# A written-out order of 2757 operations, replaced by another one: four transformer-like layers on one core

## The chip, the cores and the metric

The kernel runs on one core of one Trainium2 chip. The metric is device time in microseconds of one execution: the median of several runs. A core has five instruction queues that run side by side and meet only at semaphores: PE (TensorE, the matrix unit; its weight loads are shown apart as PEld), DVE (VectorE), ACT (ScalarE), POOL (GpSimd), and SP (SyncE), which in this kernel issues nearly all DMAs.

## The reference

The input is X, 2048 rows of 512 numbers (bf16). It passes through A, B, A, B, each with a residual: x + A(layernorm(x)), x + B(layernorm(x)). Both have 32 heads of 16 numbers.

```python
# A: causal attention inside each segment of 512 rows, and a linear memory of the earlier ones
for s in range(4):
    p = softmax(qs @ ks.T * scale + mask)
    a_dot = p @ vs
    a_mem = (phi(qs) @ M) / (phi(qs) @ z + 1e-6)     # phi(t) = t + 1 if t > 0 else exp(t)
    o = g * a_mem + (1 - g) * a_dot
    M = M + phi(ks).T @ vs;  z = z + sum(phi(ks))
# B: linear attention over all 2048 rows
pq, pk = q @ w_phi, k @ w_phi
phi_q, phi_k = [softmax(pq), softmax(-pq)], [softmax(pk), softmax(-pk)]
o = (phi_q @ (phi_k.T @ v)) / (phi_q @ sum(phi_k) + 1e-6)
# each ends with o @ wo
```

## The kernel before, in words

X stays on the chip as 16 tiles of 128 rows. A segment s (of 0 to 3) is four tiles, and L (0 or 1) counts the two A-and-B pairs. Segments of the second pair are called xA4 to xA7 in this text where their transposed input is meant, so xA5 is segment 1 of L = 1.

*Normalisation and transpose* (`ln`, line 574 on). Each tile gets its mean and variance on DVE, a reciprocal root on POOL (on ACT for the first four tiles), and a normalised copy `xn` on DVE or ACT (line 597 on DVE). Then the copy is transposed into a tile of `pX`, which holds one segment: by PE for some tiles, by a DMA transpose on SP (`tr`, line 364) for the others. The segment-1 tiles of the first pair, 4 to 7, go by DMA.

*Projections* (`a_proj`, matmuls at line 341 through `pair`). A segment's transposed input times the key, query and value weights (`WA_k`, `WA_q`, `WA_v`), two groups of four heads' pairs at a time. Keys are copied from PSUM (`Kev`) and written four times with masks (`kmask`, line 647, tile `KM`), so that one matmul can take several heads; queries are copied (`Qev`) into `QT`. The value tile is copied into `pV`, and two DMAs (line 736) make a copy with swapped halves, `pW`. For the memory, phi of the keys is transposed by DMA and multiplied with the values (`Macc`, `Mmask`).

*Attention* (`a_att`). A block is two tiles of query rows (i0 = 0 or 2) of one segment: 16 blocks in the whole kernel. For each of four head groups PE makes score groups in PSUM (line 326, tiles `pK` and `pQ`), ACT takes an exponential of each of them (line 351, some 0.8 to 1.0 us each; `exp`, `expf`, `expd`), and PE multiplies the result with the values. The causal mask is added by one matmul of `tri` with `two`. DVE divides, adds the memory's part, the result is transposed (mostly by DMA), multiplied with `WA_o` and added to X (line 925).

*Linear attention* (`b_keys` after each segment, `b_query` for each segment after the last). The key and query weights of B are folded with `w_phi` on the chip (`fold_weights`): raw weights are loaded, transposed by DMA on SP, multiplied, and copied. `Zev` copies the query normaliser out of PSUM.

*Order.* The program first lists all operations with what they read and write (`Graph.op`). Nothing schedules them as the kernel runs, and nothing plans them as it is built: the table `ORDER`, a compressed string, holds one sequence of all 2757 operations, an engine for each operation, and a buffer number for each tile. `Graph.place` (line 137) reads it and refuses an order in which an operation stands ahead of one that it needs, or a tile ahead of the end of the last user of its buffer; `Graph.emit` cuts the sequence into the five queues and puts a semaphore wait where an operation needs one on another engine. Each engine works through its queue strictly in the table's order. Buffer pools are small: five tiles of `pX` (used for xA, xB and raw weights), four PSUM tiles of 128 x 1024 (`pD`), 22 of 128 x 1024 in bf16 (`p2`).

On SP the head of the queue is, in this order: X tiles 2 and 3, X 4 to 7, the two halves of `WA_k`, beta, two parts of `WB_o`, a half of `WA_q`, a part of `WA_o`, `WB_o`, `WA_o`, `WA_v`, X 8 to 11, the transpose of tile 7, X 12 to 15, the transpose of tile 5, the raw value weights (512 KB), the transpose of tile 4, the raw key weights (512 KB), and the transpose of tile 6.

Of the kernel before, what the change touches and what calls it, by code (L numbers as in the profile page):

```python
# [16 lines left out]
D = 512  # L17
H = 32
# [3 lines left out]
NG = 4  # L22
# [275 lines left out]
class Kernel:  # L298
# [147 lines left out]
    def T(self, pool, cls):  # L446
        return Tile(pool, cls)
# [727 lines left out]
YY-J&>lKKN9Y8dp$l|{_>chNK|)9h3KBs|NCpU1p)3F}RD+^W4vK*T0s$IgKx~i@1d$L37OF#Wr~xIQJmiI%kPq@h0jK~ap%#>af>03(K_#dSb)XxRhVD=X3PWZ19;  # L1175
!eO=n1``2#kbuFbYOPdYA^|U;^}prO*dPz#DiA26Dk2$O)<7G2DfBkQTmy_wX(J08ii^+=r)-9iBlBcmXfr0gQzVkQ*k#c*qLRVGMi)51}u-f&w@gmqC9R0Lx($yoM
oI5C_3F7>*-wJB-B5PzXoi8YqlgU=s9$fv^LHz)BblA@Cz~#p%!yyJ07s0b5}*{DP}tEzE>Zm=VHZD0~fJ@CZWTJJ<=k;ByFu0LXz^@F!RTIWa3{!=GU&YRrzqushC
!9%yh51n~!$4XYqAWCM%Eu^8sTT$m4YV^7SBQy@R~!jJF^Oobvi7KcG+EQ;fBK74}VumDQnI+z83nV=-@h9tNLRzOnhi+dp%B6dNC<FOx3z~nd@*I)`9gKKdWPR0Q^
1?R#-U|bJ`De)UzjU#9gOvK*UA4gIjTnyi0W+;tia07gY-{VG@gzIoWl*a=w2-jl;+<*g7^9uwz2!?;aH~11QBfZ6`m<OieaUeq8h&8bm#>J{w4a;IVjEC{@M-0F$@
CuKCz&bbsD`7>PiPf<(*1#$ljKiol*2Q|b1w-&NI0>n-6xK)L2ABYc(^lMuoA4Zj;yXMKU%+<Uj7#tg%%U$L63@a<_%nXMKum-QF@pC&I39u%FdZAB#E;0d6lc>;+=  # L1180
cUS2QI=!I3E||9Gr`daRDyGCK!eh7=%sH@oRjKvv4=g#%WZTmSII&i7T)ORiYWR95d2%nn`nLE@h$sPK<jn2JXdRZibnuIkv!-7|E^i2(-ZvW^Rj7+zv<4XevwjC_j
~>0u)A@s32{o;uKDWs67^?Q&55g6{9FTM2AVzX^5bhs4xOzLMq&ct*`?s+Cckp5N)K&RE5e@NjiX$RDl9$FvY?%co0uuAjP1Q_!)kVhwv~4Q4BtUr*Ive#ZnXpW8-=
{hhu0geSzty8l|VIG>%GB8OlJRd=v#&ry4Y#T2d>@fXyi*wxBdPfhJN~JcgMtiX^AQwlsv=QB#^iQ)wtQqq<a&CR2TCO>L+F)uzVOgw{|UYDn{_5ly1Clo`)sdaOx?
j)JByu|0L5j&vH2V<5+cT9lPK(R{j&3uqB7p&NJsFXAO!NQ>zv-p1s#ly=ZEN<rIbIqjsBbQm1PBuim@3-90xT1hdvGaaEWbQibNQCdY^DVS#S9KMVr`3inUqj(E_P
O)eo#ina`72{BRN<?v~8}*^S6a`u6B7{&Z4rj&paVs65{j`Vn(lI(n$7wg6pa(dbAL2>6hhum;pQY1Og3r({n!zQx9G{}cn2^fzBTP-_C;^?Pew3XnaSkrVmAN>_=A
j&ib8=$pPCckU^`s;em*dfD8pbm@5vQVAT!AZcVt$Upc?5rj@i_^np|3F+SLbSc8In>c72%>>maFnaeu4*i5?A3e{1nG?DK5>2cmk)TUi1ZhNzbqb51^Xdo7QtKUdS
7G5%1^xe1HpZZXU~Xc`8riaa@q+aUssb11T9@g2J4Tlkx?c!bkZSFXknDkuFg@zDc*J887F_JfEBMU~a%GcmX%$AzY8^^D<t`OSu(i;C0-Z5AzYO#VdIgU#8W3g%WT
b&d8fN6W8VYw1pdUBW}ShxeY&{w%ml<aZ_&3pL0r1#hLjbo#MyTNHi9==_*~LJ9L+>Qx;CnDYyf7<W8KLbJ0o8O?fCi-++z$8E2#Hw3RQwJ*v(5xHISFSg?j~&?deK
X*nzBphxtC&hl|S#|^|bKEVw|7v9NTc{}gor?i82b189}&+uLj5c{~acus+$f~Y9=a5<5a(s4HK#(nubf5H8@KM&wE{3Uni9^8|A@mCZfz9uWmi)R!moQM)J#6ZqV-
_W<zn_p0v2p2Eu6@`d6B2;K$#4Q*mVu{!ySOkff;yW5H>WB+Gi2LwucujG|_Y_ZD<hr7sxWvswebHQ8<|}-QuW~g(qJ@y+4Y8;$9&jb`kcDU|DvP(IL=(|QT!U*IUt  # L1190
EXVe4X#`UB1UPMGetblo5~k9W@nC_&rq-Wkpr-1C0`+MQhPX)Do>kVo_T><)7$BYA4!@&LW9ODw2s`D4|FsK2d4`e1jiz8j)UP5XnVKkxKkbX~hTXA~J~-BBMwrGK(
zYBV`rYM0Sxt+~=E|Lv$76#1;6O$BPM~hj_+c@kG&6Jm+utD)bRAd4%XIMv52wEx+P!qPr*|a*AFemw3&+#rIrNbP%~k9+6iR5^p%4$S(?r!s0tFB8rM)Vvv|Bn#g{
lzZfE#$^l}q7$b&?vEnT^lkfQ*H<ts&4?IOo7L&w}{8UU6)5Q!iQ*;z@pr9x&W{GEFwpb$Oh@bdp{=iGcbMcj!E9Qx1V!l`|R)_^+p;#$aiI2QaeB$+DyZD6{iN#{I
SR>Yo4Pui3u~BRmD9(tpVuxrU&xtR@VX<2r5qm^SxkYRh+r&|^SL_$(#ZIwH>=OsXA#qR~7stex;)1v+E{P86vgoKDidM3<ydqAB&&5e`N<0!*#WnGnxFhb0)8d}EE
^de?@}_toZj1ZkmguB9tH<JN@j`qno``S6OYus)7T<~Q#T(H^eiTn-TiIT=lRt=GL<jjy{wO-ix1y7LC!WjB^1b*Zy2!8O*HX$h3S?XLja0I${7H0^D1R1Ceh^xID_
_f3@`ZdUhs*9VK=zO$<ae^C43uM}kz*yvAlXiRFRf(RU%rv;)c`qCj*{bKupBRid@DobXgNXllD%c9MAcnc)m3#--Bg&IC@0A{GF--$?_`7=DBsI?GE&BuQ8JB8E0f
3=GO0`_)5`=hrpzFJkO^fnnOvrj8D&c8R1Za}r}|O$Qa{N=GL}pw6U)gmwfrD6$=Gs`{8?s}ALVovtg^^KDyy8K2CIUyiYz3v$q<!W7M6WvZ`D_>lmUv>FEW?>Bv;8
m)ko!&*<}v7TCS0cWM37kgjy@B%E7Xq93t<l1bV0pQ;TIkHB45M4^%?^wW=;N=^FC3`bK5e{nZ^cKoya9)jd^I7L%ZYlvGRPQn^g7lQrcOIa^MZbL3n(P0o|k<#IVt
<&}A42{~VulIvwHSzCsyr)s!TDxKD9gi5cUsfu#EnxIz58FGP~DUF(`O3LDLq?)BhsWNh*oFyyC%JPMZr@vJZD!zWMzEY7Yk$$8K>zC@WdZnJIhbpnoprcei8AH8R-
>JQ_h|Z`>>U}ba&ZSG~q&m0WAY-cia-y1~hNz(`g-)sC=#4V2F0QZ3Ec%8lp|k2MvbHWQ>*)AuliVzC%48~=zACTD{IY<YtVXM0>U(ut&Q@FHHhD`<QQ37eom_91Q&  # L1200
nDFN9NHvbSj-jr`2_3PJKYWQ>pcPHBD`iWo0>8PbOD8Wm=U^tyKxsFY1#Tqh9K<iu5bZI=}uw<<mRlI8{KeQw8;p>WzA<=BVm=u98~l8X7d}pVjyJC-qU4)=F#rLCs
UUWO|iBB~*#jdX+-OQYqC2HD7I1TU176bSh<aY_&|y({FScJzt-fWpz1SUVkBr>I%A;J|g3&#44_;FO#S*<srFMZByG-O<hYLl^0}1U0E;Em2_3TSXa}_)dICpEmFt
iXEL?gp$^JSYLmJocgsD}>7*)+DlaR@%qpHLqyzK<9jF)T&*dFiMX%C#WsqL1?#b19jb5vl>ScPlUZI!hx_YBtsT=AIdc9t!>*@Nsk#3+*%M&tEpOib*ad}EEQJeH;
eOKSpP4sQuKsMG5Wix$WH`T#9N*|VuWQdM$n(G!iRL9UU^$N98h3UpJmOdjd%F8lb-_do{1D(LU*N=5w^+f-mU+XODJN;I_(^*wLl}*jmv-E8JRL{``)lEHD-_p-?Z
uPT%t_!J{=7au9$1?TRL)}0XR(aJHokO+M=j3J;q0h?LdX;LZ9_erN11Zfz`9goKizsCt$vo=5T&?n{oa#p%*L>8i^iMjTiEUczIHs5?s@muRs*&2N^Q!<8Xg=w0^)
3zOfY#<0y<7Lx2emOr^ikbQ_tu?t7u{B)X{WpDZo0khpvmM?9d&lqT_4hibzfao9oN;=F?~XB(<k)~-A7kf{q%OdQ#Vn2^$OEe?a?dEe!Wj8HO<r@o!Ioyo%Cn=bIs
<Iek_ZtnyRrnt#_$4YN_h4lNoD*%wRoGCo#chfOck>PG}OD;ktwhGb41k8KrBeA$q7Tsgj!%CennMk-C&RqgR=;I@IhitIbXmWn!47rkP1)mYI|$!n8G`^*McBmsMZ
r)FzE7qe`o^X1Ten+MDL)ifU)Z=oY4<>0rj{PUf0gVy>&DrktvvuByxWhN`8m=-TRmX=6H@)~2!PYPy*&=74!<nwZ_{pxI;gnmwwOS!Y_BL#n(=XN1|Sx|<$mz1d|B
tNx~**=+`x`evMNVA7j==Dt~Ej;Mp`kU4BJn8hZeIiM=49A=+6X119v=D0ay_M7eItQoHxnxkfonV^rVwWg8DWG3pIW|FR?zSI}=MV;AfFdNM|v&n2VL(O?J%p5Vj&
# [61 lines left out]
```

## Time and profile before

| | before |
|---|---|
| median of 3 runs | 477.54 us (476.16 to 478.46) |
| profiled execution, its own time | 477.2 us |
| span of the profiled execution | 475.5 us |
| mean granted TensorE clock | 0.996 of full speed |
| busy: PE, ACT, DVE, POOL | 450.5, 424.1, 418.5, 54.7 us |

The profile is of one execution. The span runs from its first instruction to its last; the execution's own time has 1.7 us more around it. An engine is busy while it works on an instruction; a share of the span is a mean over stages that are limited by different things, so it has to be read stage by stage. In rows of single instructions the number in brackets is the idle time of that engine just ahead of it, and after the arrow stands the engine, tile and line that the profile holds for the last thing waited for. A wait for several things is put down to the one that came last by its records.

### The profile page before, as it was taken

Reading aid. Unit: us, or ns where it says so; the run is one execution under the profiler, and the core shown is the slowest. Engines: PE = TensorE matmul, PEld = TensorE weight load, DVE = VectorE, ACT = ScalarE, POOL = GpSimd, SP = SyncE. Lnnn points to the kernel's source line nnn. Section 1 sums busy time; section 2 is a strip of 40 time slices with the busy share of each in tenths; the row PEclk is TensorE's granted clock in tenths of the full one; section 3 lists DMA queues with packets and bytes.
Section 4 is the critical chain, followed back from the end, with each engine's and each line's share of the span. In section 5 each row is a group of like instructions: output and inputs, shape, how many; then the busy total and the mean of one; then the engine's idle time right before and its main releaser. Section 6 shows DMA issues by size and latency. Waiting matters only on the chain.

```text
span 475.5 us, 25072 instructions
## 1 busy us (share of the span) xinstructions
PE 450.5 (95%) x11583; PEld 296.2 (62%) x11583; DVE 418.5 (88%) x812; ACT 424.1 (89%) x567; POOL 54.7 (12%) x139
## 2 busy tenths in 40 slices
PE   9979999999999999999999999999999999999885
PEld 4447665767667676565555666666666667666542
DVE  6969999999699888987999998998897887898994
ACT  3869999999999998579999999999999999786961
POOL 2301112001011101100220041110020020110000
PEclk9989999999999999999999999999999999999999
DMA  9941292352423132100133334343104404100256
GB/s 233 248 84 39 42 127 56 76 66 48 69 51 60 25 42 33 24 1 4 37 80 70 81 47 72 69 71 59 26 5 81 61 4 70 37 12 3 55 81 204
DMA packets 89388, 30.36 MB, mean 64 GB/s; under 512 B 75954, under 2 KB 89282, under 8 KB 89282
## 3 DMA queue, kind: packets, MB, share of 16 engines
q1 hardware_dynamic: 88450, 28.20, 32.0%
q8 instruction: 91, 1.49, 1.3%
q10 hardware_dynamic: 800, 0.52, 0.4%
q14 instruction: 15, 0.12, 0.1%
q0 software_dynamic: 32, 0.02, 0.0%
HBM read 6.31 MB, written 2.10 MB: 18 GB/s over the span
## 4 chain that ended last, share of the span: by engine, by line
PE 64%; ACT 21%; DVE 12%; issue 2%; POOL 1%; DVEq 0%
PE D L341 40%; PE D L326 21%; ACT p L351 10%; ACT pF L351 7%; ACT pE L351 3%; DVE p L1087 2%; PE D L662 2%; DVE p L1084 2%; DVE X L925 1%; DVE p L360 1%; DVE p L1090 1%; DVE pT L1007 1%; DVE pK L360 1%; PE D L378 1%; DVE pV L360 1%
## 5 line engine op out<-in xcount | busy, mean ns | idle before, releaser
L351 ACT ACTIVATE p<-D 128x1024 bf16<-128x1024 f32 (+1 forms) x220 | 217.5, 1018 | 12.8 <-PE D L341 7.8
L351 ACT ACTIVATE pF<-D 128x896 bf16<-128x896 f32 x128 | 115.7, 927 | 5.1 <-PE D L326 4.5
L326 PE MATMUL D<-pK,pQ 64*128 64x256 bf16 (+3 forms) x1536 | 113.7, 243 | 4.3 <-ACT pF L351 1.9
L326 PEld LDWEIGHTS D<-pK,pQ 64*128 64x128 bf16 x1536 | 55.4, 94 | 40.8 <-ACT p L351 5.2
L326 PE MATMUL D<-pV,pF 64*128 64x34 bf16 x1024 | 76.5, 176 | 1.6 <-issue 0.8
L326 PE MATMUL D<-pW,pF 64*128 64x34 bf16 x1024 | 73.9, 176 | 0.0
L326 PEld LDWEIGHTS D<-pV,pF 64*128 64x128 bf16 x1024 | 57.2, 93 | 5.8 <-ACT pF L351 2.1
L588 POOL TENSOR_SCALAR rstd<-mv 128x1 f32<-128x1 f32 x60 | 15.0, 256 | 359.7 <-DVE mv L581 359.5
L326 PEld LDWEIGHTS D<-pW,pF 64*128 64x128 bf16 x1024 | 53.5, 93 | 1.4
L326 PE MATMUL D<-pV,p 64*128 64x34 bf16 x1024 | 53.1, 176 | 0.6 <-issue 0.2
L351 ACT ACTIVATE pE<-D 128x768 bf16<-128x768 f32 x64 | 52.1, 821 | 1.5 <-PE D L326 0.9
L326 PE MATMUL D<-pW,p 64*128 64x34 bf16 x1024 | 51.7, 176 | 0.0
L326 PEld LDWEIGHTS D<-pV,p 64*128 64x128 bf16 x1024 | 47.0, 93 | 3.3 <-issue 0.7
L326 PEld LDWEIGHTS D<-pW,p 64*128 64x128 bf16 x1024 | 45.4, 93 | 1.6
L326 PE MATMUL D<-tri,two 64*128 64x128 bf16 (+1 forms) x384 | 46.2, 234 | 0.2 <-issue 0.2
L326 PE MATMUL D<-pV,pE 64*128 64x34 bf16 x512 | 45.0, 175 | 0.0
L580 DVE BATCH_NORM_STATS2 stats<-X 128x6 f32<-128x512 bf16 x64 | 43.2, 682 | 2.0 <-DMA X<-in_A_x_dram 1.7
L326 PE MATMUL D<-pW,pE 64*128 64x34 bf16 x512 | 43.2, 175 | 0.3 <-issue 0.3
L341 PE MATMUL D<-pX,WA_k 64*128 64x512 bf16 x256 | 37.3, 383 | 2.8 <-ACT pF L351 2.6
L972 DVE TENSOR_REDUCE pS<-p 128x64 f32<-128x1024 bf16 (+1 forms) x36 | 38.5, 1090 | 1.4 <-ACT p L351 1.2
L925 DVE TENSOR_TENSOR X<-X,D 128x1024 bf16<-128x1024 bf16 (+1 forms) x29 | 32.0, 1107 | 8.4 <-PE D L341 8.3
L341 PE MATMUL D<-pX,WA_q 64*128 64x512 bf16 x256 | 37.6, 384 | 0.6 <-DVE pV L360 0.5
(132 smaller groups left out, 992.3 us busy)
## 6 DMA issues: line engine op xcount, KB each, us to landing
pW<-pV SPq DMA_DIRECT2D x16, 136.0 KB, 3.6
out_dram<-X SPq DMA_DIRECT2D x7, 256.0 KB, 4.2
X<-in_A_x_dram SPq DMA_DIRECT2D x3, 512.0 KB, 5.7
pX<-in_B_wqkv_dram SPq DMA_DIRECT2D x3, 512.0 KB, 5.0
p<-p SPq DMA_TRANSPOSE x76, 2.7
pX<-p SPq DMA_TRANSPOSE x54, 3.3
WA_k<-in_A_wk_dram SPq DMA_DIRECT2D x2, 256.0 KB, 6.8
WB_o<-in_B_wo_dram SPq DMA_DIRECT2D x8, 64.0 KB, 3.6
```

The source lines that it names most:

```text
L326: ins = e.matmul(out_ap, lhsT, rhs, start=st, stop=sp, tile_position=(basep(lhsT), basep(out_ap)))
L341: ins = e.matmul(out_ap, lhsT[64 * hf:64 * hf + 64], rhs[64 * hf:64 * hf + 64], start=k == 0 and i == 0, stop=k == 1 and i == len(lists[hf ...
L351: return self.g.op({"act": (dur, lambda e: e.activation(out_ap(), in_ap(), func, scale=scale))}, reads, writes, opens, label=label)
L360: "dve": ((340 if fast else n / 0.96 + 65), lambda e: e.tensor_copy(out_ap(), in_ap()))}
L378: ins = e.transpose(pb()[:, k * 128:(k + 1) * 128], src()[:, k * 128:(k + 1) * 128], self.ident[:])
L580: v(lambda e: e.bn_stats(self.stats[:, t, :], self.X[:, t, :]), 602, [R("X", t)], [R("st", t)], label="bn")
L588: v(lambda e: e.tensor_scalar(rs, self.mv[:, t, 1:2], LN_EPS, None, op0=ALU.add), 170, [R("mv", t)], [R("rstd", t)], eng="pool", label="rstd")
L662: ins = e.matmul(D.t[c0:, r0 * 8:r0 * 8 + n], r[:, c0:], ones(r, n), start=True, stop=True, tile_position=(r0, c0))
L925: self.v(lambda e: e.tensor_tensor(X(), X(), src(), ALU.add), 65 + 512 * n / 0.96, pr + xr, xr, label="res")
L972: fn = lambda e, sgn=sgn, eo=eo, Z=Z, n=n: e.tensor_reduce(Z.t[:, 0:64 * n].rearrange("p (k s h) -> p k s h", k=n, s=2)[:, :, sgn, :], eo( ...
L1084: v(lambda e, Ns=Ns, Tm=Tm, w=w, shape=shape: e.tensor_tensor(shape(Tm.t[:]), shape(Ns.t[:]), w(), ALU.mult), 600, [Ns, AB[0], AB[1]], [Tm ...
L1087: v(lambda e, N=N, Tm=Tm, w=w, shape=shape: e.tensor_tensor(shape(Tm.t[:]), shape(N.t[:]), w(), ALU.mult), 1131, [N, AB[0], AB[1]], [Tm], ...
```

## The change

The table is replaced; not a line of the program differs otherwise. In both tables each operation stands once, and the count per queue is the same: 1055 on PE, 812 on DVE, 568 on ACT, 187 on SP, 135 on POOL.

What differs in the decoded tables:

- Fourteen operations change between DVE and ACT, seven each way. From DVE to ACT: two evacuations of PE transposes (`xnTe`, one in each pair's first segment), the normalised copy of tile 3, two key copies `Kev` (segments 0 and 1 of the first pair), one `Macc`, and the `Zev` of the last segment. From ACT to DVE: two `xnTe`, one mask piece `Km`, two query copies `Qev`, one `Kev` in the second pair, and one of the last residual evacuations (`res`).
- Within a queue an operation moves by 2.1 places on average on PE (35 at most), 1.4 on ACT, 5.2 on DVE (78 at most), 2.6 on POOL and 4.3 on SP (65 at most).
- The head of SP's queue becomes: X 2 and 3, beta, X 4 to 7, a half of `WA_k`, `WA_v`, the other half of `WA_k`, a half of `WA_q`, X 12 to 15, X 8 to 11, the transposes of tiles 5, 7, 6 and 4, then the raw key weights, two `pW` copies, parts of `WB_o` and `WA_o`, the raw query weights and the transposes of raw key weights. The raw value weights go from place 16 to place 33.
- On PE, the first score group of rows 2 and 3 of segment 0 (third head group) goes ahead of the key projection of segment 1, and its exponential ahead of another one on ACT.
- In segment xA5 the normalisations of tiles 36 and 39 (tiles 4 and 7 of X in the second pair) stand behind 2.1 and 5.6 us more work on DVE; in xA6 two stand behind 5.2 and 6.2 us more; in xA3 the last one behind some 6 us less.

```diff
 ORDER = """
-c-rlH1GHt=vUXwmSZ&+3ZQHhO+qP}nM$$~$HiJge2)fh%+WRDV$-T+D_l@zt@ngKT_gQnzxvFYbeO2>YYmR-ALkdU(bs;q*fqGCM8bCv61dX8yG=*l+99lq2Xa%jI4
...
+c-rlH1Gr_!w(dZATW#C6ZQHhO+qP}nwvslJ?xc;Nku-vSbFJOU3C_9qyzhJW>AQ39wdSmvRipm#kAI9+bFZBoQa~E03-zErG=PTC2pU6tXaY^488n9$&=Oif5=a0EK
...
 """
```

More of the change, by code (lines that the diff above doesn't have):

```diff
@@ L1178 @@
[L1178 to L1193, printed above, removed]
@@ new lines @@
+=V>BJdEtfeerc9zi^K3{M~%WQ5o7Eqn=2;SJn{GB6TG!DyHOW8oS606)S#_zto|4wwexU_5*Uxxhef$O&&@3`~OF&<Fa$_wWw-!$24TOJOh;!euZ73*#Vo317ni=m*
+Q;K5T+*&=p7Gc31<Wup0*PO2`U3U^Q%p;Wz@fKmja>TOkCV!wOghLtr8dhFAC=Ucmzhg`KbqI^uN5fmv_{bi$mN6=%W{m<_+;T3Cgv@dISTpI|6z%#Pi07|w$pXmB$
+83`4=<I>?K8Fdyc}+?WfCV^16g<FN=9!=l&=C*WutgAV7zdKeCXC2$r@fvHdulVD%m4P$W+B*g{rEBpd`A(-btKU{;!aU3G9#m<-lKf*#thI4^2CBDNhH~>e`B%Fx7
+aRc<nk<<q_LTOwC>u?ah#}~L5%HVq359RRy48#ps0ViWwoPrxM69ghMab`FOS>PjngRhZrDt^G9@LT*2r(sQui{-EuR>f*K1LNUL{2q@(1joln{uwm~U}da=)v*Rv!
@@ new lines @@
+a7(RgRvqmz`9ru=U@U1!TM;p0Rka0hj1vr!6^O#V=z%DMnWJ&zzMhtC*c&tg4B2#N?`y5K`>0mhPV*t;wHQRTW~XO#m`_HehxA4B5cQDbPmqLa9V=9aTm_Roj8q_;(
+VM=jc^vtrp7o6BQOyr#2+yxhht*g2LhXTu7<%&`~~0QY+R0ua2f8vid2{u;|g4fqo@)Uq0y9)X3$K^L_v56!muf}#y!{!EjPy&=y)$iVjFCW?JzU7#P(R0%27TFqx=
++w1?UVEq&YN~&O#vyr=qlpiqU3@AVI~c1Z^Nm8%g3mOocHqfMeky+K+?i0CvDu7zbmcLPdFCFdf7bcnDA8VK_{Y6hKv|6qTgXRG!XZ8Cpjb=sb?0YP6oxQB|r;>FEN
+FrO#25p~G06YS1Y>jTz_&9!0?|sTDP+G?*60Q41PR>F^ky!3;QoGGaSwOG9WPWx_C?LUm~>4W)Y2l$y~bnoPB+4%MeN)SA{%LuyP7s0lTqd9;=?V-OvIK&nX>@iROM
@@ new lines @@
+mvBC{rw-JSqDZo(U^)h8@i^9^P85qnDK5l@KvtZE!ucjHpj)_z7Se58OkZGfT1F{o8!e&bw1bw?cG^OhaVKr1JD8GUkfRl}l2X%`*qLT?7dk>+sSjPjIee7v;#C~Uq
+xc%`qgZr|V$)Z+pN>-;x`Ey3I(DbNlpbSJ59&w#sV5DfRn&_v!4=p=yXh32roD86_Rs-3OJ`^_pQM8{hVS9mIGyif2|h>XX$F_%gp{3&aSl#E@u)YgrmPe~5AgwBpw
+B2Le@=-gE*0lg6q_q?WuD1#cqq@}VH}s^Qz9<M<vB4|;EMbdhx0QW!AUqiKga4^jf-$muF40w3?Jf0IFTRYB#y^vC?O}~wDbfA(nX2`rTHkA<tluP^Yd6P#fhl~*W@
+HrfXDH8&czFPF6ZV6yol#<L7vR(c`6s;X}p1xavm<s3HTE2=L6h~FH>_~%u{$iFXt<ioCos|PQghj3NAx3iUCWw0k7Z%+>q;WeO|_`cqy;t4BVR6@nO!$b$BJO;;WR
@@ new lines @@
+2uhDh7K{qK2*W%iIo9@sN-pqCRE84<sxGlHfmi#p}=BC_8wBttHgxhmUPQ{t|J~b8(sRMW9PQ02=^GUu1srd`~l5WEpKE=7{IOnEpw2@EnCeBWI=q_dD^qhkp&?CxA
+IVlZy=38`+)^I+~%R6}&U*L1Rl^ck&yp6l?cHYhBxuGa0y7CTwOyxx>v5)s~fY{63xI6dY&-in;qO=GUPsxdAR6$e}&nZGgi6;~(Vu)`kOoWT?=z9tgp(3`>!iZPYm
+wWO>?#F5Q8|u%!xHk{rf&7B9aV!y2+<_obM+A#6ARWgM!^9=N%!9ZOzofV#o~SE^i+bV;R}xqG8eiwvR9{pUB&vyKLJAhu#n;?I2+>@$6mRH0-+*iIfR(rj@x=|k$=
+Bfrdc<u+P0>~~5j8{^(NvTbKhj&OBHqy`QB{l<twk%*Nz@ieMJ@4|@9-D=CEw)_^qy|<J#Hu3i_RjU_?420L?W?BB0f@T0sN4EqVyt-$RJXP<RX<wD}JUfB9q7{Qi^
@@ new lines @@
+mUv&bTTp%LN<cNJMhHj!N<5MS|a&LN(2H!)7U;F01PcNgQuQ~s8};R)h9o+x^W-r{@iBl?OdqJ$VAriz^6CBNp9qJwzFJw#8DOXL=XL>^IC<P~qYh$t%ZiTt9NC?J~
+1exj)yBl?T6Vvraj28zMr9S;?g#U$~bAB$;Xx|ktmijJbVC@7lAAGo>vk>Bzx@kGoPOT--U6Mx{R;+goFmx{S!o>(U4iv?n#ST0tGMdBA;CqD9ev0ePiE5$0YSj2?Y
+VvSfUHi%6E#741Mpg1SaixzT+xF9|kTf|neO&k`x#SyVbw3J81Ua?<X6g$N(u}>Tj2gM<AOk5VnMF(|7+!t3xN7YKUme<4yaax=dXT$^XnYbiwi0k5%_)^>zXT?2nQ
+`{1d<Zbb__(I$fUx`ktvwA2ViEqTW;)QrFz7yYzcCxMfMZ6TR#B1?J{3;&HHnP2ZB0I<*L`V6fcqZQoDWA(u^1V><seB>dijShR{NQc;P<D}BWjFbgXrq1>T6UM;NG
@@ L1233 @@
+QnsjX)R!BV6r^(fDRCsa@B-ojF&Ctq;FL&c#UH(oM_c)2Jvc!St@xGhIog#Q6-6`vv
 """
```

80 lines of the change are left out of this document (38 added, 42 removed).

## The prediction

> **What bounds the kernel now.** I read the page's totals first, then the busy times of six stretches, which I cut where the character of the work changes, and last the instruction rows of the one stretch with idle time in it. In the stretch rows the columns are: window, its length, busy time and (instructions) of PE, PEld, DVE, ACT and POOL, the granted TensorE clock, the DMA share and GB/s.
>
> ```profile
> span 475.5 us, 25072 instructions
> PE 450.5 (95%) x11583; PEld 296.2 (62%) x11583; DVE 418.5 (88%) x812; ACT 424.1 (89%) x567; POOL 54.7 (12%) x139
> ...
> 0.00:40.00 40.00, 35.88 (x491) 19.46 (x493) 31.11 (x93) 26.92 (x43) 7.09 (x27) 0.96 0.73 168
> 40.00:180.00 140.00, 135.14 (x3986) 94.89 (x3982) 126.24 (x225) 138.18 (x178) 16.38 (x40) 1.00 0.36 60
> 180.00:220.00 40.00, 39.13 (x878) 24.40 (x876) 34.21 (x64) 30.10 (x45) 3.14 (x8) 1.00 0.11 18
> 220.00:400.00 180.00, 173.56 (x4796) 116.63 (x4792) 163.01 (x322) 177.26 (x228) 25.02 (x56) 1.00 0.30 53
> 400.00:440.00 40.00, 39.64 (x864) 25.40 (x860) 35.50 (x60) 31.01 (x44) 3.06 (x8) 1.00 0.14 25
> 440.00:475.50 35.50, 27.19 (x598) 15.43 (x592) 28.45 (x53) 20.63 (x34) 0.00 (x0) 0.99 0.49 114
> ```
>
> PE has the largest total, but in the two long stretches ACT is the full engine: 138.18 of 140 us and 177.26 of 180. In 180 to 220 and 400 to 440 PE is full and ACT has 9.9 and 9.0 us to spare. Only the first 40 us are short of both, and only there is the clock below 0.99. As the next stretch is bound by ACT, a microsecond that ACT gains in the first 40 is carried along, until a later wait eats it.
>
> The loss in the first 40 us sits in one place. The next rows are windows around it, then PE's, ACT's and DVE's instructions there (start, length, engine and line, operation, tiles; in brackets the idle time ahead of it and what the profile names as its end).
>
> ```profile
> 23.70:26.40 2.70, 0.05 (x4) 0.04 (x3) 2.12 (x7) 1.70 (x3) 0.00 (x0) 1.00 1.05 177
> 27.70:31.20 3.50, 3.50 (x22) 1.69 (x20) 1.97 (x5) 2.46 (x3) 0.00 (x0) 0.51 0.49 111
> ...
> 23.52 0.22 PE L326 MATMUL D<-tri,two 64*128 64x128 bf16 x2
> 26.39 1.04 PE L341 MATMUL D<-pX,WA_k 64*128 64x512 bf16 x8 [2.65 <-ACT pF L351]
> 29.39 1.92 PE L341 MATMUL D<-pX,WA_q 64*128 64x512 bf16 x8
> 31.37 1.04 PE L341 MATMUL D<-pX,WA_q 64*128 64x512 bf16 x8
> ...
> 27.71 0.92 ACT L351 ACTIVATE pF<-D 128x896 bf16<-128x896 f32 x1 [2.32 <-PE D L326]
> 29.66 1.02 ACT L351 ACTIVATE p<-D 128x1024 bf16<-128x1024 f32 x1 [1.03 <-PE D L326]
> 31.56 1.02 ACT L351 ACTIVATE p<-D 128x1024 bf16<-128x1024 f32 x1 [0.36 <-PE D L326]
> 33.20 2.54 ACT L351 ACTIVATE pF<-D 128x896 bf16<-128x896 f32 x3 [0.62 <-PE D L326]
> ...
> 29.23 1.23 DVE L360 CAST p<-D 128x1024 bf16<-128x1024 f32 x1 [3.41 <-PE D L341]
> ```
>
> PE stands still for 2.65 us ahead of the key projection of segment 1, and then runs at a granted clock of 0.51 for 3.5 us (the same eight matmuls take 1.92 us there and 1.04 after). ACT loses 2.32 + 1.03 + 0.36 + 0.62 = 4.33 us behind it, DVE at least 3.41. The profile names an exp as the releaser, but that projection also needs the transpose of the last tile of segment 1, which SP issues:
>
> ```profile
> 14.63 0.57 SPq L457 DMA_DIRECT2D X<-in_A_x_dram  x1
> 17.14 0.59 SPq L457 DMA_DIRECT2D pX<-in_B_wqkv_dram  x1
> 19.01 0.58 SPq L457 DMA_DIRECT2D pX<-in_B_wqkv_dram  x1
> 19.64 1.32 SPq L364 DMA_TRANSPOSE pX<-p  x1
> ...
> pX<-in_B_wqkv_dram SPq DMA_DIRECT2D x2, 512.0 KB, 5.1
> pX<-p SPq DMA_TRANSPOSE x1, 6.5
> pX<-pX SPq DMA_TRANSPOSE x2, 2.5
> ```
>
> The first four rows are SP's instructions, the last three the medians from issue to landing. The transpose issued at 19.64 landed 6.5 us later, at about 26.2, which is when PE went on (26.39). With nothing large ahead of it, two transposes from 27 us on landed in 2.5. Ahead of it stood two raw weights of 512 KB (issued at 17.14 and 19.01, 5.1 us each). So the first stall is a transpose behind two loads that nobody needs yet.
>
> **The change part by part.** Only the table changes. All 2757 operations stay, with the same count on each engine, so no busy time is added or removed but by the 14 evacuations, normalisations and mask pieces that swap DVE for ACT, half each way; their ACT work nets to about 0.6 us less by the rows of their forms, which I count inside the stretches below.
>
> *The loads at the head.* In the new table SP issues the two X loads and the attention weights first, then the four transposes of segment 1 in one group, and only then the raw key and value weights (raw value was 16th on SP, now 33rd); the output weights, first used near 58 us and 215 us, follow. The four transposes have no large load ahead of them that is not needed itself. With 2.5 to 5 us to landing instead of 6.5, and X 12 to 15 loaded earlier, the last one lands before PE comes to it. Removed: the wait of 2.65 us. Removed with it: the halved clock, 3.5 us at 0.51, so 3.5 x 0.49 = 1.7 us. Sum −4.35, which agrees with the 4.33 us that ACT loses there. Moved later are the raw weights: they are folded behind 27 us and used by the linear-attention block after that; the transposes of raw weights have the empty queue of 27 to 31 us (2.5) as cover. If that cover fails, the fold comes late, but its first user lies behind the first eight exps of the next block, some 8 us: I cost it at nothing.
>
> *What is late next.* The new PE order puts the first score group of rows 2 and 3 ahead of the segment-1 projection, so at about 23.7 PE waits for that group's last mask piece on DVE instead.
>
> ```profile
> 0.00:25.90 25.90, 22.57 (x247) 11.10 (x247) 21.40 (x69) 16.68 (x30) 7.09 (x27) 1.00 1.01 237
> ```
>
> DVE had worked 21.40 us when that mask piece ended, at 25.8. In the new order 18.8 us of DVE work stand ahead of it (the same rows summed by the new table), 2.6 less, so it ends near 23.2 if DVE waits no more than now, and up to 1 us later if it waits for its inputs as before. Bounds 0 and +1.0; I take +0.6, the size of the two short ACT waits above (0.36, 0.62). Whether so short a wait halves the clock is no term: the 0.51 followed 2.65 us.
>
> The Trainium skill, page "TensorE: Matmul & The Clock Gate", section "Part 1: The HAM clock gate", says the clock falls to half after an idle window of about 3.4 us that runs free of the kernel. By that rule a wait of 2.65 us need not have cost any clock, while the trace has the halved stretch right behind it, and its length of 3.5 us agrees with the page's window. Were the halving not tied to this wait, the 1.7 us would stay; that is rival E.
>
> *Segment xA5 of the second attention layer.* DVE's normalisations for this segment stand behind 2.1 us (tile 36) and 5.6 us (tile 39) more DVE work than before.
>
> ```profile
> 250.51 0.74 DVE L597 TENSOR_SCALAR p<-X,mv,rstd 128x512 bf16<-128x512 bf16 x2
> 249.62 4.71 SPq L364 DMA_TRANSPOSE pX<-p  x3
> pX<-p SPq DMA_TRANSPOSE x1, 3.3
> 256.66 1.04 PE L341 MATMUL D<-pX,WA_q 64*128 64x512 bf16 x8
> ```
>
> The last transpose, issued near 252.3, landed 3.3 us later, at about 255.5; its projection began at 256.66. The slack is about 1.15 us. A tile that is last by 2.1 us costs 2.1 − 1.15 = 0.95. Bounds: 0, if the added DVE work fills time in which DVE now waits, and 5.6 − 1.15 = 4.45 less the 1.22 us of the residual add that DVE now does later, 3.2. I take 0.95, because the tile delayed by 5.6 us is no longer the last to be transposed. Segment xA6 has the same kind of shift (5.2 and 6.2), but it lies where PE is the full engine; I cost it at 0, bounds 0 and 1.
>
> *The two long stretches.* PE's places move by 2.1 on average, ACT's by 1.4, DVE's by 5.2, and the work ahead of each PE operation stays within 1 to 4 us. The exps there can only win what ACT waits for now, in the rows below (us in total, times, longest; 40 to 180 first, then 220 to 400):
>
> ```profile
> ACT p L351 <- PE D L326: 0.5, 3, 0.2
> ...
> ACT pF L351 <- PE D L326: 1.1, 3, 0.6
> ACT p L351 <- PE D L326: 0.4, 1, 0.4
> ACT pX L359 <- PE D L378: 0.2, 1, 0.2
> ```
>
> All its waits come to 0.9 and 1.7 us, 2.6 in all: that is the gain's bound. The loss has no row; its bound is rival D's +7. I take 0, by these rows: in 406 ACT instructions of the two stretches the waits are few and single, and a shift by two places on average leaves most scores where they were.
>
> *The tail.* The last copy of the query normaliser goes from DVE to ACT, and one of the last residual evacuations from ACT to DVE:
>
> ```profile
> 440.17 0.69 DVE L360 COPY p<-D 128x512 f32<-128x512 f32 x1
> 440.80 0.29 DVE L1065 TENSOR_TENSOR pS<-pS 128x128 bf16<-128x128 bf16 x1
> 471.02 1.22 DVE L925 TENSOR_TENSOR X<-X,D 128x1024 bf16<-128x1024 bf16 x1 [3.40 <-PE D L341]
> ```
>
> After the copy (0.69) DVE works on without a wait, on the operand that ACT now has to copy first, and ahead of its last residual add DVE waits 3.40 us for PE, more than one evacuation (1.22). Cost 0, bounds −0.5 and +0.5.
>
> *Sum.* −2.65 − 1.70 + 0.60 + 0.95 + 0 + 0 = −2.8 us. The profiled execution took 477.2 in its own time (span 475.5 and 1.7 around it); the runs' median, 477.54, is 0.34 above it. 477.2 − 2.8 = **474.4**, on the median's footing 474.7; I give 474.4.
>
> **Rivals.**
> A, the forecast: 474.4, of itself between 472.8 (no mask wait and no xA5 wait, 1.55 less) and 476.2 (mask wait 1.0 and 1.4 more at xA5).
> B, the whole stall comes back and the stretches give half of their 2.6 us: 477.2 − 4.35 − 1.3 = 471.5. For it: the new table has 0.6 us less ACT work where ACT is the bound. Against: PE's new first group wants a mask piece.
> C, the gain is given back in the stretches: ACT runs 2.8 us ahead of its old time, and transposes that were just in time (slack 1.15 at 256.66) are now asked for earlier, while their queue is no faster: about 477.
> D, slower: PE's and ACT's orders are shifted on their own (2.1 and 1.4 places), so exps are starved of scores once in each attention block. Sixteen blocks lie in the two layers; at 0.6, the longest wait of the 220 to 400 row, they cost 9.6, less the 2.6 that is there now, +7: 474.4 + 7 = 481.4. It decides from 0.35 us a block (5.6 in all). For it: no row of before shows how much slack the exps have. Against: ACT waited for 2.6 us in 320 with an order just as tight.
> E, the halved clock stays for another reason: 474.4 + 1.7 = 476.1.
>
> **How the numbers follow.** About 0.5% (2.39 us) is what a measurement of this kernel tells from no change: faster is below 475.15, slower above 479.93. A has 0.42 (0.30 of it below 475.15, 0.12 above), B 0.22, C 0.11, D 0.20, E 0.05. So faster 0.30 + 0.22 = 0.52, same 0.12 + 0.11 + 0.05 = 0.28, slower 0.20. The range reaches from 471.0, half a microsecond below B, to 480.0, which leaves out most of D; A's own range is 472.8 to 476.2.
>
> **What would show it.** Right: between 20 and 34 us no PE wait above 1 us and a clock of 1.00 throughout; the transposes of segment 1 land within 5 us of issue; ACT busy in 0 to 40 rises from 26.92 by about 3.5. At the projection of xA5 near 253, a PE or ACT wait of about 1 us. In the long stretches ACT's waits stay near 0.9 and 1.7. Wrong: a wait above 2 us at the head before the first score group of rows 2 and 3 (the mask piece, not the transpose, was the limit), with the clock at half behind it; or ACT waits in the long stretches that grow by several us, which would be D; or PE waiting for xA5's last tile for more than 2 us.

## The result, and the profile after

| | before | after |
|---|---|---|
| median | 477.18 us (476.16 to 478.46, 7 runs) | 472.89 us (472.56 to 475.04, 7 runs) |
| ratio, 95% interval | | 0.9924 [0.9902, 0.9945] |
| profiled execution, own time | 477.2 us | 473.13 us |
| span | 475.5 us | 471.3 us |

The change makes the kernel 4.3 us faster (2.6 to 4.7 by the interval). 474.4 was forecast, with 472.8 to 476.2 as the likeliest case's own range; 472.89 lies at its lower end.

The page's totals and the six stretches of the changed kernel, in the columns of the prediction (the last stretch is shorter, as the span is):

```profile
span 471.3 us, 25089 instructions
PE 448.9 (95%) x11583; PEld 296.5 (63%) x11583; DVE 419.8 (89%) x812; ACT 423.1 (90%) x567; POOL 56.8 (12%) x139
...
0.00:40.00 40.00, 38.67 (x636) 21.36 (x637) 34.48 (x100) 31.68 (x48) 7.39 (x28) 1.00 0.60 161
40.00:180.00 140.00, 135.97 (x3986) 94.61 (x3985) 127.36 (x223) 137.59 (x177) 16.87 (x40) 1.00 0.38 63
180.00:220.00 40.00, 38.31 (x882) 24.92 (x880) 35.01 (x69) 31.17 (x49) 3.30 (x8) 1.00 0.07 14
220.00:400.00 180.00, 174.19 (x4805) 117.75 (x4803) 161.22 (x315) 175.90 (x225) 26.18 (x56) 1.00 0.31 55
400.00:440.00 40.00, 38.52 (x862) 24.44 (x856) 36.80 (x68) 30.78 (x48) 3.03 (x8) 1.00 0.09 19
440.00:471.30 31.30, 23.23 (x432) 13.42 (x428) 24.92 (x42) 15.98 (x25) 0.00 (x0) 0.97 0.53 124
```

In the first 40 us ACT worked 31.68 us instead of 26.92, 4.8 more, and the clock is 1.00. In the long stretches ACT is still the full engine, but a little less so: 137.59 of 140 (138.18 before), 175.90 of 180 (177.26).

The place of the first stall, as windows, and then PE, ACT and SP there:

```profile
23.70:26.40 2.70, 2.70 (x36) 1.40 (x33) 2.70 (x8) 2.70 (x5) 0.00 (x0) 1.00 0.42 94
27.70:31.20 3.50, 3.48 (x113) 2.45 (x111) 3.38 (x7) 3.44 (x5) 0.00 (x0) 1.00 0.88 209
...
24.54 0.38 PE L326 MATMUL D<-pK,pQ 64*128 64x256 bf16 x4
24.85 1.04 PE L341 MATMUL D<-pX,WA_k 64*128 64x512 bf16 x8
...
25.37 1.05 ACT L351 ACTIVATE p<-D 128x1024 bf16<-128x1024 f32 x1
...
14.81 5.67 SPq L364 DMA_TRANSPOSE pX<-p  x4
20.52 0.58 SPq L457 DMA_DIRECT2D pX<-in_B_wqkv_dram  x1
...
pX<-p SPq DMA_TRANSPOSE x3, 2.5
```

All three engines are busy through both windows. The four transposes go out one behind the other, the last of them land 2.5 us after their issue, and the raw key load (20.52) follows them. The score group of rows 2 and 3 goes at 24.54 without a wait, the key projection of segment 1 at 24.85 instead of 26.39.

The next list is worked out from the traces: how far PE is ahead of the profiled execution of before, in us, when it has done the same number of operations. It is counted from the first operation behind the warm-up matmuls, because that one starts at another time in each execution (its start is in the first row).

```
operations done (time in before)  after   loads moved  new head   new first   old first half,
                                          in old order  only       half only   new second half
start of the first (before 7.94)   8.64    9.54          8.98       8.58        9.07
  88 (42 us)                       -4.5    -4.0          -4.6       -4.5        -2.9
 180 (80 us)                       -6.3    -4.2          -3.9       -6.0        -3.3
 360 (152 us)                      -6.0    -2.9          -2.7       -5.7        -2.9
 490 (212 us)                      -6.5    -3.0          -2.9       -5.6        -2.9
 630 (278 us)                      -5.2    -2.7          -2.9       -5.6        -1.4
 966 (419 us)                      -6.1    -2.3          -2.9       -5.0        -1.1
1020 (446 us)                      -5.2    -2.3          -2.9       -5.0        +0.9
 end                               -5.2    -2.3          -2.9       -5.0        +0.8
```

By this list the head brings 4.5 us, the next 170 us another 2, and from 212 us on 1.3 are given back, 0.9 of them near 440 us. But the same number of operations is not the same operations where the order differs. Timed by the same exponentials on ACT and counted from the same start (the median of those of 40 to 60 us of before, of 140 to 160, and of 400 to 420), after is 5.2, 5.9 and 6.1 us ahead, and the run with the loads moved in the old order 3.9, 2.9 and 2.3. So between 60 and 160 us the new order adds 0.7 us, where the old one gives back 1.0.

### The profile page after: what moved, and what is told of

Read it like the earlier page. It is cut to its first block, busy times and chain, and to the rows that moved or that the text cites. A ratio compares the mean times of both kernels' runs of the same rounds, so it can differ in the third digit from the quotient of the medians.

```text
span 471.3 us, 25089 instructions
## 1 busy us (share of the span) xinstructions
PE 448.9 (95%) x11583; PEld 296.5 (63%) x11583; DVE 419.8 (89%) x812; ACT 423.1 (90%) x567; POOL 56.8 (12%) x139
## 4 chain that ended last, share of the span: by engine, by line
PE 56%; ACT 31%; DVE 9%; issue 2%; POOL 1%; DVEq 0%
PE D L341 37%; PE D L326 17%; ACT p L351 16%; ACT pF L351 9%; ACT pE L351 4%; PE D L662 2%; ACT pS L351 1%; DVE X L925 1%; DVE stats L580 1%; DVE p L874 1%; DVE p L1084 1%; PE D L378 1%; DVE p L597 1%; POOL rstd L590 1%; DVE p L791 1%
## 5 line engine op out<-in xcount | busy, mean ns | idle before, releaser
L326 PE MATMUL D<-pV,pF 64*128 64x34 bf16 x1024 | 75.5, 176 | 1.2 <-ACT pF L351 0.8
L588 POOL TENSOR_SCALAR rstd<-mv 128x1 f32<-128x1 f32 x60 | 17.5, 297 | 352.6 <-DVE mv L581 349.7
L590 POOL TENSOR_TENSOR rstd<-rstd,mhalf 128x1 f32<-128x1 f32 x60 | 36.7, 625 | 3.3
```

The source lines that it names most:

```text
L326: ins = e.matmul(out_ap, lhsT, rhs, start=st, stop=sp, tile_position=(basep(lhsT), basep(out_ap)))
L588: v(lambda e: e.tensor_scalar(rs, self.mv[:, t, 1:2], LN_EPS, None, op0=ALU.add), 170, [R("mv", t)], [R("rstd", t)], eng="pool", label="rstd")
L590: v(lambda e: e.tensor_tensor(rs, rs, self.mhalf[:], ALU.pow), 540, [R("rstd", t), R("mhalf")], [R("rstd", t)], eng="pool", label="rstd")
```

## The experiments

Each kernel has the same operations and differs only in the decoded table. The diffs show the decoded order. In all spliced orders the operations that the first part has already issued are left out of the second, each operation keeps the engine of the order it comes from, and buffers follow that order's succession.

### The two raw loads, in the old order

```diff
 SP, order of before:
   transpose tile 5
-  load raw v (512 KB)
   transpose tile 4
-  load raw k (512 KB)
   transpose tile 6
+  load raw v (512 KB)
+  load raw k (512 KB)
```

> The order of before with one edit on SP's queue: the raw value and raw key weight loads (512 KB each) go from between the transposes of segment 1 to just behind the last of them. Theory (the head's loads): the last transpose lands near 22.5 us instead of 26.2, PE's wait of 2.65 us and the halved clock behind it go, and the time falls by about 4.3 us, to 472.9 (from 477.2). Rival (the wait is the one that the profile names, an exp that frees a PSUM tile): the wait stays above 1 us and the time is within 1 us of 477.2. Rival (the gain comes from the order of the rest): no more than 1 us faster.

Measured: 475.03 us (10 runs), ratio 0.9956 [0.9930, 0.9981]. So 2.1 us faster, not 4.3. The stall is gone (the rows are of PE's and ACT's waits between 15 and 40 us, then of ACT's waits between 40 and 180 us, with us in total, times, longest):

```profile
PE D L341 <- ACT pF L351: 0.3, 1, 0.3
PE D L326 <- issue: 0.3, 1, 0.3
...
ACT pF L351 <- PE D L326: 1.0, 3, 0.5
ACT p L351 <- PE D L326: 0.8, 3, 0.4
ACT pE L351 <- PE D L326: 0.2, 1, 0.2
```

The largest PE wait at the head is 0.3 us, and the clock is 1.00 throughout the first 40 us, so the 2.65 and the 1.7 went with the loads; PE is 4.0 us ahead at 42 us. But 1.7 us are gone at the end. ACT's waits in the next stretch add up to 2.0 us (0.9 before): exps that come earlier now wait for scores that PE still makes in the old order:

```profile
84.25 0.92 ACT L351 ACTIVATE pF<-D 128x896 bf16<-128x896 f32 x1 [0.51 <-PE D L326]
87.93 0.92 ACT L351 ACTIVATE pF<-D 128x896 bf16<-128x896 f32 x1 [0.34 <-PE D L326]
```

That is what rival C of the prediction says, a gain given back in the stretches, though here the exps wait for scores and not for transposes. ACT's waits have grown by 1.1 us in all; the other 0.6 of the 1.7 has no row here.

With only the raw key load moved:

```diff
 SP, order of before:
   load raw v (512 KB)
   transpose tile 4
-  load raw k (512 KB)
   transpose tile 6
+  load raw k (512 KB)
```

> The order of before with only the raw key load moved behind the last transpose; the raw value load stays ahead. Theory (each 512 KB load ahead costs the transpose about its own transfer, some 2 us between landings): the last transpose lands near 24.2 us, PE's wait is 0 to 0.6 us and nothing follows it; 475.0 to 475.5, as with both moved. Rival (one load is enough to keep the stall): a wait above 1.2 us, 476 to 477.

Measured: 475.59 us (10 runs), ratio 0.9947 [0.9919, 0.9974], the same as with both within the intervals. The last transpose landed at 23.86, the projection began at 24.11, and the largest PE wait there is 0.33 us. So the rival is refuted: the raw value load alone, which still stands ahead, does not make the stall, and the raw key load behind it is what brings the landing to 26.19. The key load without the value load was not tried.

### The loads put back, in the new order

```diff
 SP, order of after:
   transpose tile 6
+  load raw k (512 KB)
+  load WA_o, four parts (128 KB each)
   transpose tile 4
-  load raw k (512 KB)
 ...
-  load WA_o, four parts
```

> The order of after with one edit on SP's queue: the raw key load (512 KB) and the four loads of attention output weights (128 KB each), together as much as the two raw loads that stood there before, go ahead of the last transpose of segment 1. Theory (the head's loads): that transpose lands 4 to 6 us later, PE waits 1.5 to 3 us ahead of the key projection of segment 1, the clock halves behind it, and the time goes up by 2.5 to 4.7 us, to 475.5 to 477.5. Rival (the rest of the order): within 1 us of 472.9.

Measured: 476.92 us (10 runs), ratio 1.0003 [0.9976, 1.0030]. By the medians the whole gain is gone with this one edit. PE waits again, and here the profile names the transfer:

```profile
27.77 1.04 PE L341 MATMUL D<-pX,WA_k 64*128 64x512 bf16 x8 [2.25 <-DMA pX<-p]
```

The transpose behind the loads landed at 27.72, later than in before (26.19), so the stall is a larger one. The halved clock that was expected behind the wait did not come there; it came at 439.94. Counted as in the list above, this execution is 2.2 us ahead of before at 42 us, 4.2 at 212 and 2.3 at the end, where after is 4.5, 6.5 and 5.2 ahead: 2.3 us went with the loads, and near 440 us it lost 2.0 where after lost 0.9. So by the medians the order of the loads is worth about 2 us in the old order and 4 in the new one, but the 4 are not all shown to be the stall.

### Pieces of the two orders

First the second half alone, and the last query stage alone:

```diff
-order of before: all
+order of before up to PE operation 490 (212 us), then order of after
```

> The order of before up to the last query projection of the first pair (some 212 us), then the order of after. Theory (the head carries it all): no faster than before; as the profile of after is 5.7 us ahead of before at that point and only 4.2 at the end, the second half costs 1.5 us: about 478.7. Rival (the second half's order is better too, the 1.5 is chance of one execution): 476 to 477.2.

Measured: 479.77 us (12 runs), ratio 1.0058 [1.0030, 1.0086]: slower by 2.8 us. The direction is the theory's, the size nearly twice its 1.5. In its profile PE loses most near 440 us, where the clock halves (below).

```diff
-order of after: all
+order of after up to PE operation 998 (436 us), then order of before
```

> The order of after up to 436 us (all but the last query stage), then the order of before. Theory (the tail of the new order gives back 1.2 us, as the two profiles are 5.4 us apart at 430 us and 4.2 at the end): about 471.7. Rival (a chance of one execution): 472.9, as after.

Measured: 473.37 us (12 runs), ratio 0.9927 [0.9900, 0.9955]. That is the changed kernel's own ratio; the 1.2 us did not come.

```diff
-order of after: all
+order of after up to PE operation 490 (206 us), then order of before
```

> The order of after up to some 206 us (the last query projection of the first pair), then the order of before. Theory (the second half of the new order costs): the order of before with the new second half took 2.8 us more than before, so taking the new second half out of after gains as much: 472.9 - 2.8 = 470.1. Rival (the second half costs only behind the old first half, where DMAs and waits stand otherwise): 472.9, as after. Rival (the old second half loses what it is given, because its transposes were just in time): 474 or more.

Measured: 472.60 us (6 runs), ratio 0.9903 [0.9871, 0.9936]. The expected 470.1 is missed: what the new second half costs behind the old first half (2.8 us) it does not cost behind the new one. Beside the changed kernel once more:

> The order of after up to some 206 us, then of before, once more beside the changed kernel. Theory (the new second half brings nothing): one group of times near 472.5, at or below the changed kernel's median. Rival (the new second half gains): 0.5 us or more above it.

Measured: 472.98 us (8 runs, 471.68 to 476.63), ratio 0.9913 [0.9879, 0.9947], in place of one narrow group: five times are 471.7 to 473.1, three 475.4 to 476.6. The second half of the new order neither gains nor costs anything that these runs can tell.

```diff
-order of before: all
+order of after up to PE operation 88 (38 us), then order of before
```

> The order of after up to some 38 us (through the first attention blocks' scores), then the order of before. Theory (the head carries two thirds): in the traces, counted from the first operation behind the warm-up matmuls, after is 4.7 us ahead of before at that point and 6.4 at 183 us. If the old rest keeps that, 477 - 4.7 = 472.3, less what a typical execution of before does not lose at the head. Rival (the old rest gives gains back, as in the run with the two raw loads moved, where 4.0 us at 40 us became 2.3 at the end): 474.5 to 475.5.

Measured: 474.81 us (12 runs), ratio 0.9954 [0.9927, 0.9981], the value of the run with the two loads moved. The rest of the new head (the score group ahead of the projection, the engines) adds nothing that can be measured when the old order follows, as the rival had it; the splice itself adds two ACT waits of 0.5 us near 40 us. On the same chip, the run with the new first half took 472.60, and its highest time (472.94) lies under the lowest one here (473.36): behind the new head, the new order up to 212 us is worth some 2 us.

```diff
-order of before: all
+order of before up to PE operation 88, order of after up to 490, then order of before
```

> The order of before, with the order of after between some 41 and 212 us only. Theory (the middle of the new order is better by itself, 1.7 us in the traces): 475.3. Rival (the middle only gains where the head has been shortened): 477.

Measured: 484.53 us (6 runs), ratio 1.0138 [1.0089, 1.0187]. Neither theory had this. PE waits 3.44 us at the old place and then for the folding of the key weights:

```profile
28.15 1.04 PE L341 MATMUL D<-pX,WA_k 64*128 64x512 bf16 x8 [3.44 <-issue]
...
52.95 1.03 PE L341 MATMUL D<-pX,WA_k 64*128 64x512 bf16 x8
59.13 0.60 PE L326 MATMUL D<-p,pX 128*128 128x128 bf16 x4 [4.91 <-DMA pX<-pX]
...
54.08 3.81 SPq L364 DMA_TRANSPOSE pX<-pX  x3
```

SP had been through its work at 32.4 and then stood until 54.08, at the transpose of the raw query weights, with those of the raw keys behind it. The five buffers of `pX` are the cause: the old head has loaded the raw value weights at 17 us, and so the transposed query weights get the buffer of segment 1's input, which is free only when its last projection, begun at 52.95, is through. The new head leaves the raw value weights for later (52 us) and had these transposes out from 27.63 on. The new middle is not better by itself; it is made for the new head, by a buffer as much as by a queue.

```diff
-order of after: all
+order of after up to PE operation 490, order of before up to 966 (413 us), then order of after
```

> The order of after, but with the order of before from some 206 to 413 us (all the second pair up to the last key projections of its linear attention). Theory (the last 60 us of the new order cost 0.8 to 1.2 us, more where the clock halves there): 0.8 to 1.5 us slower than the run that has the old order for the whole second half. Rival (the loss lies before 413 us): the same as that run.

Measured: 474.19 us (12 runs), ratio 0.9939 [0.9912, 0.9967], 1.2 to 1.6 us above the two medians of the run with the old second half. The intervals overlap. Six of its times are 472.3 to 473.5 and six 474.9 to 476.6.

```diff
-order of after: all
+order of after up to PE operation 966 (413 us), then order of before
```

> The order of after up to some 413 us, then the order of before (an earlier cut than 436 us, ahead of the stretch where PE waits 0.50, 0.60 and 0.81 us within 8 us). Theory (those waits, and the halved clock that they bring in some executions, are all that the tail costs): one group of times near 472.0, 0.5 to 1 us under the changed kernel. Rival (the tails cost the same): as the changed kernel.

Measured: 472.78 us (6 runs, 471.94 to 474.34), ratio 0.9893 [0.9858, 0.9928].

> The changed kernel once more, beside the next two on the same chip, to have its spread. Theory (in the last 40 us the clock halves in some executions, for one window of 3.4 us): times in two groups about 2 us apart, near 472.8 and 475. Rival (the spread comes from the warm-up at the start alone): one group, no wider than 1.7 us.

Measured: 473.89 us (8 runs), ratio 0.9920 [0.9888, 0.9951]; the times are 472.86 to 474.75 and one of 477.0, not two groups. The variant without the new tail is 1.1 us lower in the median beside it, with overlapping intervals. No version was shown to beat the changed kernel; the one with the old last 60 us has the lowest ratio.

## Why the prediction was right, point by point

**The wait (−2.65) and the halved clock (−1.70).** Both happened, as the windows of after show, and the cause was the one named: with the loads put back the wait returns, with them moved in the old order it goes. But the size is that of one execution. In three executions of the old head (before, the one with the new second half, the one with the new middle) PE waited 2.65, 1.45 and 3.44 us, and the clock halved behind the first alone. The second is this row:

```profile
26.33 1.04 PE L341 MATMUL D<-pX,WA_k 64*128 64x512 bf16 x8 [1.45 <-ACT pE L351]
```

In the first two the last transpose landed at 26.19 and 26.08, although PE's first operation behind the warm-up came at 7.94 and 9.07, so the late start ate up a part of the stall; in the third it landed at 27.95. The loads alone are worth 2.1 us in the median, not 4.35.

The granted clock on record for each execution says when the 4.35 is right. A half-speed window of 3.41 us takes the mean over the execution to 0.996 or less. Of 77 executions of before beside the experiments, 22 are at 0.996 or less, and all of them took 478.2 us or more (median 479.0); the other 55 took 476.6 in the median. Of the executions with both loads moved (10), with the new head alone (12) and with the key load alone moved (10), none, none and 2 are at 0.996 or less. Of those of before on the chip of the run with the loads moved (475.03), 9 with such a window took 478.9 in the median and 24 without it 476.4: the loads are worth 3.8 us against the one and 1.4 against the other. (The mean does not say where the window lay, and a half-speed stretch behind PE's last work counts in it too.) The forecast was built on an execution that had the window, which fewer than a third have; its early start (7.94; the fourteen profiles start at 7.90 to 9.54) makes up for a part of that in its time of 477.2.

**The mask piece (+0.60).** It was not paid. The piece ended at 23.84, the group went at 24.54, as soon as PE was free of the projection ahead of it. Lower bound 0 was right. One reading was wrong: what ended at 25.8 in before is a statistics instruction of a normalisation (line 580), not a mask piece; the two pieces that this group waits for last ended there at 30.98 and 37.94.

**xA5 (+0.95).** It was not paid either. The last of its transposes landed at 250.45, and PE took the projection of its queries at 252.68:

```profile
252.68 1.04 PE L341 MATMUL D<-pX,WA_q 64*128 64x512 bf16 x8 [0.27 <-ACT p L351]
...
247.45 0.41 DVE L597 TENSOR_SCALAR p<-X,mv,rstd 128x512 bf16<-128x512 bf16 x1
...
242.96 6.31 SPq L364 DMA_TRANSPOSE pX<-p  x4
```

The wait is 0.27 and for an exp. The slack went from 1.15 to 2.2 us, although the normalisations did come later, measured against the projection (which is 3.98 us earlier than in before): that of tile 36 ends at 247.85 instead of 251.25, 0.6 later by this measure, and that of tile 39 at 245.94 instead of 245.51, 4.4 later. What the forecast left out is the way from there. In before two tiles were ready within 0.3 us; the last transpose went out 1.0 us after its tile was ready and landed 3.3 us after that. In the new order the tiles come one by one, the last transpose goes out at once (247.88) and lands 2.6 us later. That wins back 1.7 us. Why 2.1 us of added work made tile 36 late by 0.6 only is not shown.

**The two long stretches (0).** In the first the new order gained 2 us beyond the head by the count of operations (0.7 by the same exponentials), where none was counted, and it did not give back what the old order gives back; this is the term that was too small, and with the loads' gain it makes up the 4.3. By which operations it does so is not shown. ACT's waits grew all the same, from 0.9 to 1.6 us in the first stretch and from 1.7 to 3.1 in the second, whose rows follow behind those of the first:

```profile
ACT pE L351 <- PE D L326: 0.7, 1, 0.7
ACT pF L351 <- PE D L326: 0.6, 2, 0.4
ACT p L351 <- PE D L326: 0.3, 1, 0.3
...
ACT pF L351 <- PE D L326: 1.4, 2, 0.8
ACT p L351 <- PE D L326: 0.9, 2, 0.7
ACT pE L351 <- PE D L326: 0.5, 2, 0.3
ACT pS L778 <- PE D L326: 0.3, 1, 0.3
```

Rival D had this mechanism at 9.6 us in all; the waits grew by 2.1.

**The tail (0, bounds −0.5 and +0.5).** It cost 0.9 us in the profile, outside the bounds. The copy that goes to ACT was weighed on its own, but not with the groups (`N`, B's queries times the summed keys and values) that were moved on PE around it; they wait for ACT, whose copy is the last row:

```profile
435.88 0.41 PE L326 MATMUL D<-Rkv,p 64*128 64x64 bf16 x16 [0.60 <-ACT p L359]
436.80 0.41 PE L326 MATMUL D<-Rkv,p 64*128 64x64 bf16 x16 [0.50 <-ACT p L351]
442.98 0.65 PE L326 MATMUL D<-Rkv,p 64*128 64x64 bf16 x32 [0.81 <-ACT p L351]
...
435.25 0.58 ACT L359 ACTIVATE p<-D 128x512 f32<-128x512 f32 x1
```

The first of these groups stood ten PE operations further back in before; now it waits for the copy's end at 435.83. The second waits for the evacuation that ACT does right behind the copy, and the half of a projection that stood ahead of it on PE in before now follows it (437.25). The cost repeats: between 436 and 446 us the two profiles of the changed kernel and the one with the old order from 206 to 413 us lose 0.9 to 1.0, and those with the old order in the last 60 us lose nothing.

So the sum came out near the measurement (−2.8 against −4.2 between the two profiles) because the stall was there in full in the profile of before, which was chance, and because the errors at the middle (2 gained) and behind it (1.3 lost) are of opposite sign; that two costs, put at 1.55 together, did not come makes up most of the difference. The profile of after also started 0.7 us later (8.64 against 7.94). So the direction rests on a step that the runs confirm, the nearness of the sum in good part on luck; how the 4.3 us divide does not follow the forecast's terms. Of its own signs, those at the head came (ACT's busy time there rose by 4.8, more than 3.5), those of xA5 and of the long stretches did not. Rival C, the gain given back later, is what happens to the loads' gain in the old order (4.0 to 2.3), and does not happen with the new middle behind the new head.

What stays open: why the new second half costs 2.8 us behind the old first half and nothing behind the new one. A halved clock does not explain it: among executions with a mean clock of 0.997 or more, the old head with the new second half took 479.2 in the median (6 of its 12), before on the same chip 476.4 (24). Nor is the halving tied to the new tail alone: 7 of the 12 executions with the old order from 436 us on are at 0.996 or less, and 1 of the 15 of the changed kernel.

## What to carry to other kernels

A transfer that is needed soon should not be issued behind large ones that are needed late: two loads of 512 KB between the transposes made a stall here, one did not, and putting such loads back cost the whole gain by the medians. Of the 4.0 us that moving the loads won at the head, the old order gave 1.7 back later, so such an edit has to be tried with the order that follows it. And a stall in one profile has the size of that execution: compare it with where the transfer lands, with another execution, and with the granted clock of all executions, before it becomes a term of a sum.

## What the runs showed of the hardware

**The start differs by up to 1.6 us between executions.** The warm-up matmuls run at half speed until a moment that differs. Two rows of the same window, 4 to 7 us, in which before and then the run with both loads moved do the same warm-up:

```profile
4.00:7.00 3.00, 3.00 (x65) 1.71 (x64) 2.75 (x8) 0.85 (x5) 0.00 (x0) 1.00 1.08 328
```

```profile
4.00:7.00 3.00, 3.00 (x8) 0.91 (x6) 2.81 (x9) 0.91 (x5) 0.00 (x0) 1.00 1.07 327
```

65 matmuls against 8; most of the 65 are short ones further on in the same sequence, which the other execution reaches 1.6 us later. The clock column says 1.00 in both, so the half speed of the start is seen in the matmuls alone (0.43 us from one to the next, 0.21 later). This is one source of the spread of 1.3 us and more within each kernel's runs.

**The clock is granted in windows of 3.413 us that run from that moment.** The trace's records of the granted clock (us, the value from there on):

```
before                          1.0 from 3.85, 0.5 from 27.74 for 3.41
old head, new second half       1.0 from 6.14, 0.5 from 443.04 for 3.41
loads put back in new order     1.0 from 6.45, 0.5 from 439.94 for 3.41
old head, new middle            1.0 from 5.80, 0.5 from 57.00 for 6.83 and from 302.76 for 3.41
```

Every halving begins a whole number of 3.413 us behind the first record (7, 128, 127, 15 and 87), so a halving is to be compared with the window ahead of it. Those windows, of before, of the run with the loads put back, and of the one with the old first half, each with the stretch behind it where the clock is at half:

```profile
24.30:27.70 3.40, 1.31 (x16) 0.83 (x18) 1.52 (x6) 1.10 (x2) 0.00 (x0) 1.00 0.78 139
```

```profile
436.50:439.90 3.40, 2.12 (x102) 1.62 (x100) 2.54 (x7) 2.93 (x8) 0.00 (x0) 1.00 0.02 5
439.90:443.40 3.50, 3.50 (x79) 2.08 (x76) 3.26 (x8) 3.02 (x7) 0.00 (x0) 0.51 0.37 75
```

```profile
439.60:443.00 3.40, 2.12 (x102) 1.69 (x102) 2.58 (x7) 2.93 (x8) 0.00 (x0) 1.00 0.00 0
443.00:446.50 3.50, 3.50 (x80) 1.84 (x76) 3.41 (x8) 3.18 (x8) 0.00 (x0) 0.51 0.32 55
```

PE was busy for 2.12 of the 3.40 us ahead of two of them, in many short matmuls with waits of 0.5 to 0.8 us between. The same groups of the changed kernel fell into a window with 2.32 us busy, and its clock stayed whole; the new tail is near the edge, and where the windows fall decides whether an execution loses 1.7 us there. Busy time alone does not set the edge: the run with the loads put back had 2.02 us busy in the window from 23.5 to 26.9, in longer matmuls, and kept its clock.

In the fourteen traces together there are some 1900 such windows. Each of the ten in which PE was busy for 40% or less is followed by half speed (seven of them at the end of the program), and none in which it was busy for more than 63%. In between both occur: 51% and twice 62 to 63%, of short matmuls, lost the clock, and 45, 54, 58 and 59%, around the stall at the head, kept it. So the length of a wait alone does not tell: the 3.44 us of the run with the new middle lie across two windows, 54 and 45% busy, and cost no clock, while 2.1 of the 2.65 us of before lie in one, which is 40% busy.

The Trainium skill, page "TensorE: Matmul & The Clock Gate", section "Part 1: The HAM clock gate", has a free-running window of 3413 ns; the trace agrees to the last digit that it shows (3.413). It speaks of an idle window ahead of the halving; here windows that were 39% and 62% busy were enough, and the measurement decides.

**PE stopped once without a wait that the profile shows.** In the second profile of the changed kernel it did so in the middle of a group of eight matmuls, while the raw value load was in flight:

```profile
57.60 1.03 PE L341 MATMUL D<-WA_o,p 64*128 64x512 bf16 x7 [1.23 <-issue]
```

ACT then waited 1.53 us, and that execution took 477.0. `issue` stands for time in which the engine waits for nothing on record; that its instructions came late, because of the load or otherwise, was not tested.
